# Holding TensorE for a set of score banks, shorter key-value sums, and another order in the last layer

## The chip, the cores and the metric

The kernel runs on one core of a Trainium2 chip. The metric is the device time of one execution in microseconds (us), and smaller is better. TensorE (PE) multiplies matrices and writes PSUM, a memory of eight banks of 512 fp32 columns; ScalarE (ACT) computes functions such as exp and ln; VectorE (DVE) does elementwise work; GpSimd (POOL) and SyncE (SP) do small things and issue DMAs. Each engine takes its instructions in the order in which the program wrote them, and waits at an instruction for the semaphores of others.

## The reference

Four layers are applied to x of 2048 positions and 512 features, each as `x = x + layer(layernorm(x))`. Layers 0 and 2 are attention with 32 query heads of 16 features and one shared key and value head; layers 1 and 3 are linear attention with 32 heads. Cut to what matters:

```python
def A(x, wq, wk, wv, wo):              # layers 0 and 2, S = 2048, H = 32, Dh = 16
    q, k, v = heads(x @ wq), x @ wk, x @ wv
    scores = einsum("bhqd,bkd->bhqk", q, k) * Dh ** -0.5
    return merge(einsum("bhqk,bkd->bhqd", softmax(scores), v)) @ wo

def B(x, wqkv, wo):                    # layers 1 and 3
    q, k, v = split(x @ wqkv)
    pq, pk = phi(q), phi(k)            # phi(t) = where(t > 0, t + 1, exp(t)) + 1e-6
    kv = einsum("bhsd,bhse->bhde", pk, v)
    z = einsum("bhsd->bhd", pk)
    num = einsum("bhqd,bhde->bhqe", pq, kv)
    den = einsum("bhqd,bhd->bhq", pq, z)[..., None] + 1e-6
    return merge(num / den) @ wo
```

## The kernel before

**The plan.** The order of the instructions is not written by hand. The kernel's Python holds a planner (class `Planner`) that plays the whole program through on a clock of its own, with a cost written beside each operation (so 0.22 us for a score product, 0.051 + 0.4267 n for an exponential of n banks), and writes down for each engine the order in which operations were begun. An operation is created by `op`, which finds what it depends on, and has a priority; a smaller number goes first. Whenever an engine is free in the plan, `_dispatch1` takes the ready operation of the best priority. On the chip the engines follow these orders, with semaphores between them; the plan's clock itself is not on the chip. Steps that need a buffer are generators that ask a pool for it ("acq") and go on when they get it; `banks` is the pool of single PSUM banks, `sets` that of the score sets.

**An attention layer** (`run_a`). Positions are cut into 16 tiles of 128. For a query tile, a parity, a key tile and one of four head groups there is one block of scores, 128 keys by 512 columns; the layer has 2048 blocks. Two sets of three PSUM banks (banks 0 to 2 and 3 to 5) take turns. `act_stream` makes a round: it acquires the set that comes free (L1047 and after), lets PE write two or three blocks into it (`qk_mm`, L926, four rows of the array side by side, priority 0), and lets ACT turn two or three banks into probabilities PT in one call (L1107). PT has eight buffers. When DVE's backlog is small, the third bank goes to DVE (`dve_split`, `dve_take`): it turns the scores into an approximate exponential by one addition whose int16 result is read as bf16 (L1194), and makes three shifted copies for a chunk of up to four blocks (L1236), which are combined with fixed weights. A set is free again when ACT's call, and DVE's where there is one, are done. Bank 7 and others that are free are used in the same way for blocks of DVE alone (`alone`).

The value products (`pv_post`, `pv_try`, L980, four columns of the array side by side, priority 2.0) add up PT and DVE's results in bank 6 (`ACC`), tile by tile; DVE copies the sum out (L1259, L1261), PE transposes it (L1278), DVE divides (L1285, L1289), and the output projection and the residual addition follow. Next to all that, PE makes the projections of the neighbouring layers piece by piece (L672, L840). When PE has nothing to do in the plan, `fill` (L1025) and `fill_lin` (L911) put in matmuls on zeros that nobody reads.

A score product and a value product use the array in different modes, "row" and "col"; the planner charges 0.107 us (`SWITCH`) for a change. After the last exponential the sets are given back as single banks.

**A linear layer** (`run_b`) is worked into the attention layer before it as its tiles come: keys and values of a tile (`tile_`), phi (L1363 on ACT, L1364 and L1366 on DVE), queries (`q_`). `kv_` (layer 1) and `kvt` (layer 3) add pk times v, and the sum z, over groups of four tiles (the last groups three and one): the sums of a group are one PE operation of up to 16 matmuls per bank (L1477, L1480 and L1608), added into `kvacc` by DVE.

**The end of layer 3.** When the last tile's sums are there, DVE masks z into the block-diagonal Zbd (L1497) and kv into kvT (L1501); `mix` multiplies kvT with the output weights into four matrices M, copied from PSUM by ACT, DVE, DVE and ACT (L1517, `MCOP`). `den3` makes the denominators of one or two tiles: a product with Zbd (L1542), ln on ACT (L1545), exp of minus that on ACT (L1549, priority 0.02 ahead of the logarithm's by `EXB`), and the product with the query on DVE (L1553). `main3` multiplies by M (L672), DVE adds the residual (L1572), and SP stores the tile. Pairs of banks for `den3` are claimed by `take_pairs`, when the last sums are done.

Of the kernel before, what the change touches and what calls it, by code (L numbers as in the profile page):

```python
# [35 lines left out]
class Planner:  # L36
# [3 lines left out]
    def __init__(self, nc):  # L40
        self.nc = nc
        self.now = 0.0
        self.events = []
        self.seq = 0
        self.ready = {e: [] for e in ENGS}
        self.busy = {e: False for e in ENGS}
        self.until = {e: 0.0 for e in ENGS}
        self.order = {e: [] for e in ENGS}
        self.writer = {}
        self.readers = {}  # L50
        self.flags = {}
# [8 lines left out]
        self.near = {e: [] for e in ENGS}  # L60

    def soon(self, e, o, dur):
# [78 lines left out]
    def _dispatch(self, e):  # L141
        self._dispatch1(e)
        if e == PE and not self.busy[e] and self.idle:
            self.due = [t for t in self.due if t > self.now]
            for f in self.idle:
                f()
        if e == DV and self.hungry and (not self.ready[DV] or self.backlog(DV) < DXB):
            self.hungry[0]()

    def _dispatch1(self, e):  # L150
# [4 lines left out]
        while h:  # L155
# [9 lines left out]
            if w:  # L165
                held.append(x)
                self.at(w, lambda: self._dispatch(e))
                break
            if e == PE and STICK and o.mode != "row" and o.mode != self.mode != "row":
                like = [y for y in h if y[2].eng is None and y[2].mode == self.mode and y[0] <= o.prio + STICK]  # L170
                if like:
                    y = min(like)
                    h.remove(y)
                    heapq.heapify(h)
                    held.append(x)
                    o = y[2]
                    dur, fn = o.opts[e]
            if o.port:
                self.port = self.now + dur
# [264 lines left out]
EXB = 0.02  # L444
# [4 lines left out]
MCOP = (AC, DV, DV, AC)  # L449
# [9 lines left out]
def bass_interleave_layers__grouped_kv_mqa__linear_attn_block__prompt_kernel(  # L459
# [36 lines left out]
    ve = sb("ve", [P, T], FP32)  # L496
    rs = sb("rs", [P, T], FP32)
# [396 lines left out]
    lin = {"a": False, "done": False, "next": -1.0}  # L894

    def fill_lin():
        if pl.busy[PE] or ("x", 3, T - 1) in pl.flags:
            return
        b = ACC
        if lin["a"]:  # L900
# [16 lines left out]
    def run_a(L):  # L917
# [113 lines left out]

        def act_stream():
# [12 lines left out]
            while True:  # L1045
                s_ = yield ("acq", sets, 0.0)
                group = []  # L1047
# [61 lines left out]
                ex.begun = lambda n=n: pl.due.append(pl.now + 0.051 + 0.4267 * n + 0.17)  # L1109
# [138 lines left out]
        def norms():  # L1248
# [17 lines left out]
            lin["a"] = False  # L1266

# [89 lines left out]
    def run_b(L):  # L1357
# [76 lines left out]
        def q_(t):  # L1434
            pr = QBASE + 0.02 * t if QBASE and t >= CRIT else base(t) + 0.01 * t + 0.2
            yield ("flag", ("xnT", L, t))
# [3 lines left out]
            s_ = yield ("acq", bq_pool, pr)  # L1440
            b = yield ("acq", banks, pr)
# [5 lines left out]
        def kvt(gi, ts):  # L1447
# [19 lines left out]
            for i, (c, n) in ((1, parts[1]), (0, parts[0])):  # L1467
# [4 lines left out]
                def fn(e, i=i, b=b):  # L1472
                    ins = None
                    for g in range(4):
# [9 lines left out]
                op({PE: ((0.04 if i else 0.07) * 4 * len(ts), fn)}, reads=rd, writes=[B_(b)], prio=pr, lat=0.2).cols = (16 if i else 512) * len(ts)  # L1484
# [9 lines left out]
            if end:  # L1494
                mk = mask8[:, :, 0:DH]
                v4 = lambda x: x.rearrange("p g (h c) -> p g h c", c=DH)
                o = op({DV: (0.6, lambda e, b=bs[1]: e.tensor_tensor(  # L1497
                    out=v4(Zbd), in0=bank(b, 4).unsqueeze(2).unsqueeze(3).to_broadcast([P, 4, 8, DH]), in1=mk.unsqueeze(1).to_broadcast([P, 4, 8, DH]), op=ALU.mult))},
                       reads=["mask8"], writes=[B_(bs[1]), "Zbd"], prio=pr, after=[("FB", 11, 0)])
# [4 lines left out]
                pl.give_after(banks, bs[0], [o])  # L1504
                for g in range(4):
                    pl.process(mix(g))
            pl.flag(("kv", L, gi))

        Zbd = FB[:, 11, 0:512].rearrange("p (g c) -> p g c", c=P)
        kvT = FB[:, 11, 512:1024].rearrange("p (g c) -> p g c", c=P)  # L1510

        def mix(g):
            pr = 1.45 + 0.001 * g
            b = yield ("acq", banks, pr)
            mm(bank(b), [(kvT[:, g, :], wo2[:, g, :])], ["kvT", "wo2"], b, pr, 0.216)
            dst = FB[:, 0, g * 512:(g + 1) * 512]
            by = {AC: (0.48, lambda e: e.copy(dst, bank(b))), DV: (0.6, lambda e: e.tensor_copy(dst, bank(b)))}  # L1517
            c = op({MCOP[g]: by[MCOP[g]]} if MCOP else by, writes=[B_(b), ("FB", 0, g), ("M", g)], prio=pr)
            pl.give_after(banks, b, [c])
            pl.flag(("M", g))  # L1520

        def take_pairs():
            yield ("flag", ("kv", L, len(KVG) - 1))
            claim(PAIRS, "pair")

        def den3(ts):
# [4 lines left out]
            yield from until(*[("QT", t) for t in ts], "Zbd")  # L1531
# [6 lines left out]
            for k, t in enumerate(ts):  # L1538
# [5 lines left out]
                op({PE: (0.23, fn)}, reads=[("QT", t), "Zbd"], writes=[bk[k]], prio=pr, lat=0.2).cols = 512  # L1544
# [4 lines left out]
            op({AC: (0.148 + 0.427 * n, lambda e: e.activation(rb, rd, ACTF.Exp, scale=-1.0))}, reads=[("rd", i)], writes=[("rb", i)], prio=pr - EXB, after=[("PT", i)])  # L1549
# [27 lines left out]
        def kv_(gi, ts):  # L1577
# [19 lines left out]
            for gs in ((0, 1, 2), (3,)):  # L1597
# [6 lines left out]
                def fn(e, gs=gs, b=b):  # L1604
                    ins = None
                    for i, g in enumerate(gs):
# [3 lines left out]
                    return ins  # L1610
                rd = [("pk", t % 8) for t in ts] + [("va", t % 8) for t in ts] + [("sacc", u) for u in sorted({2 + t % 8 // 2 for t in ts})]
                o = op({PE: (0.08 * len(gs) * len(ts), fn)}, reads=rd, writes=[B_(b)], prio=pr, lat=0.2)
                o.cols = 136 * len(gs) * len(ts)
# [203 lines left out]
```

## Time and profile before

| | us |
|---|---|
| median of 3 runs | 1493.5 (1492.58 to 1494.95) |
| the profiled execution, its own time | 1491.57 |
| its span, first to last instruction | 1489.8 |
| ACT busy, in the span | 1455.9 |
| DVE busy | 1439.1 |
| PE busy, with the matmuls on zeros | 1420.3 |
| first and last attention exponential begin | 9.0 and 1453.4 |

The profile lists groups of instructions as line, engine, operation, what is written and read, shapes and count; behind the first bar the time in which at least one of the group ran and the mean length of one in ns; behind the second the idle time of the engine just before them and who ended it. An instruction's record can overlap the next one of its engine, so waits that are shorter than the overlap do not appear as idle time. In the time line, a line begins with the start and the length in us. A view by windows gives each engine's busy time in a stretch.

### The profile page before, as it was taken

The page shows a single profiled execution, that of the slowest core. Times are in us where ns is not written, and L with a number is a line of the kernel's source. Part 1 is how long each engine was busy: PE and PEld are TensorE (multiplying, and loading weights), DVE is VectorE, ACT ScalarE, POOL GpSimd, SP SyncE. Part 2 cuts the span into 40 slices and gives each one's busy share as a digit, 9 for nine tenths or more (in the row PEclk, how much of TensorE's full clock was granted, in tenths as well). Part 3 has the DMA queues.
Part 4 walks back from the last instruction along what each step waited for, and adds up shares of the span by engine and source line. Part 5 has one row for each costly group of instructions (what it writes and reads, how often), then busy time and mean ns, then how long its engine had stood idle before and what let it go on. Part 6 is the DMA issues. An engine that isn't in the chain of part 4 may idle for free.

```text
span 1489.8 us, 36266 instructions
## 1 busy us (share of the span) xinstructions
PE 1420.3 (95%) x14792; PEld 515.5 (35%) x14792; DVE 1439.1 (97%) x2679; ACT 1455.9 (98%) x1443; POOL 77.2 (5%) x155
## 2 busy tenths in 40 slices
PE   8999999999999999999999999999999999999999
PEld 4423333323323333323733333333333333333336
DVE  8899999999999999999879999999999999999996
ACT  8999999999999999999799999999999999999996
POOL 5000000000000000000022000000000000000000
PEclk9999999999999999999999999999999999999999
DMA  5100000000000000000031000000000000000001
GB/s 125 62 9 8 9 8 6 9 8 5 9 9 9 9 5 5 2 1 2 2 48 39 2 12 9 12 9 9 5 9 5 9 9 9 8 2 2 1 2 58
DMA packets 53540, 20.71 MB, mean 14 GB/s; under 512 B 47232, under 2 KB 52864, under 8 KB 53376
## 3 DMA queue, kind: packets, MB, share of 16 engines
q1 hardware_dynamic: 52320, 18.36, 5.7%
q8 instruction: 118, 1.93, 0.5%
q14 instruction: 46, 0.38, 0.1%
q10 hardware_dynamic: 1056, 0.03, 0.0%
HBM read 5.28 MB, written 2.10 MB: 5 GB/s over the span
## 4 chain that ended last, share of the span: by engine, by line
PE 21%; ACT 14%; DVE 10%; issue 5%; DMA 1%; DVEq 0%; ACTq 0%
ACT PT L1107 13%; PE ps L980 7%; PE ps L926 6%; DVE FB L1194 5%; DVE FB L1236 3%; PE ps L672 3%; PE ps L1025 2%; PE ps L840 1%; PE ps L1278 1%; DMA xnT<-xn 1%; PE ps L911 0%; ACT phE L1363 0%; DVE sacc L1259 0%; DVE QT L1366 0%; DVE st L754 0%
## 5 line engine op out<-in xcount | busy, mean ns | idle before, releaser
L1107 ACT ACTIVATE PT<-ps 128x1024 bf16<-128x1024 f32 (+1 forms) x1309 | 1399.7, 1230 | 3.9 <-PE ps L926 2.5
L1194 DVE TENSOR_SCALAR FB<-ps 128x512 int16<-128x512 f32 x1046 | 687.3, 679 | 7.0 <-PE ps L926 4.4
L926 PE MATMUL ps<-QT,KM 32*128 32x512 bf16 x4096 | 530.4, 385 | 30.3 <-ACT PT L1107 23.4
L980 PE MATMUL ps<-FB,VW 128*32 128x512 bf16 x4184 | 528.0, 385 | 16.8 <-ACT PT L1107 6.3
L1236 DVE TENSOR_SCALAR FB<-FB 128x2048 int16<-128x2048 int16 x786 | 515.3, 676 | 0.4
L980 PE MATMUL ps<-PT,V 128*32 128x512 bf16 x3050 | 482.1, 386 | 13.0 <-ACT PT L1107 9.9
L926 PEld LDWEIGHTS ps<-QT,KM 32*128 32x128 bf16 x4096 | 133.4, 91 | 433.7 <-ACT PT L1107 303.4
L980 PEld LDWEIGHTS ps<-FB,VW 128*32 128x32 bf16 x4184 | 132.1, 94 | 184.4 <-issue 83.9
L1025 PE MATMUL ps<-QT,V 128*32 128x512 bf16 (+6 forms) x758 | 178.3, 312 | 1.6 <-DVE FB L1194 1.6
L980 PEld LDWEIGHTS ps<-PT,V 128*32 128x32 bf16 x3050 | 120.7, 94 | 128.2 <-issue 60.1
L1025 PEld LDWEIGHTS ps<-QT,V 128*32 128x32 bf16 x758 | 60.3, 95 | 81.1 <-issue 51.7
L672 PE MATMUL ps<-wqkv,xnT 128*128 128x512 bf16 (+1 forms) x272 | 77.2, 372 | 0.0
L745 POOL TENSOR_TENSOR rs<-ve,mhalf 128x1 f32<-128x1 f32 x59 | 43.1, 732 | 579.6 <-DVE ve L743 575.3
L743 POOL TENSOR_SCALAR ve<-mv 128x1 f32<-128x1 f32 x32 | 14.7, 458 | 674.0 <-DVE mv L755 673.8
L1363 ACT ACTIVATE phE<-ps 128x512 bf16<-128x512 f32 (+1 forms) x66 | 42.3, 642 | 7.1 <-PE ps L840 5.5
L1278 PE MATMUL ps<-identF,sacc 128*128 128x128 f32 x256 | 46.8, 291 | 0.8 <-DVE sacc L1259 0.8
L1259 DVE COPY sacc<-ps 128x512 f32<-128x512 f32 x64 | 43.5, 679 | 1.3 <-PE ps L980 1.1
L754 DVE BATCH_NORM_STATS2 st<-x_sb 128x6 f32<-128x512 bf16 x60 | 40.5, 679 | 2.1 <-DMA x_sb<-in_A_x_dram 1.9
L840 PE MATMUL ps<-xnT,wqkv 128*128 128x128 bf16 x512 | 38.8, 220 | 0.0
L672 PE MATMUL ps<-wo,OT 128*128 128x512 bf16 x120 | 37.4, 385 | 0.0
L840 PE MATMUL ps<-xnT,wq 128*128 128x128 bf16 x464 | 36.3, 221 | 0.9 <-DVE FB L1194 0.4
L1278 PEld LDWEIGHTS ps<-identF,sacc 128*128 128x128 f32 x256 | 27.4, 141 | 22.2 <-issue 13.5
(138 smaller groups left out, 640.5 us busy)
## 6 DMA issues: line engine op xcount, KB each, us to landing
out_dram<-x_sb SPq DMA_DIRECT2D x16, 128.0 KB, 1.7
x_sb<-in_A_x_dram SPq DMA_DIRECT2D x6, 256.0 KB, 4.2
wqkv<-in_B_wqkv_dram SPq DMA_DIRECT2D x1, 1536.0 KB, 8.9
xnT<-xn SPq DMA_TRANSPOSE x48, 2.4
x_sb<-in_A_x_dram SPq DMA_DIRECT2D x4, 128.0 KB, 2.5
wq<-in_A_wq_dram SPq DMA_DIRECT2D x1, 512.0 KB, 4.1
wo<-in_A_wo_dram SPq DMA_DIRECT2D x1, 512.0 KB, 4.1
wo<-in_B_wo_dram SPq DMA_DIRECT2D x1, 512.0 KB, 9.6
```

What stands on the lines that cost most here:

```text
L672: return e.matmul(dst, lhsT=l, rhs=r, start=(k == 0), stop=(k == len(pairs) - 1))
L745: op({PO: (0.55, lambda e: e.tensor_tensor(out=rs[:, t:t + 1], in0=ve[:, t:t + 1], in1=mhalf[:], op=ALU.pow))}, reads=[("ve", t), "mhalf"] ...
L840: ins = e.matmul(dst[:, g * P:(g + 1) * P], lhsT=lhs(g, k), rhs=rhs(k), start=(k == 0), stop=(k == FT - 1))
L926: return e.matmul(bank(b), lhsT=KM[r, sg.par, kt * P:(kt + 1) * P], rhs=QT[r, sg.t, :], start=True, stop=True)
L980: ins = e.matmul(ps[32 * j:32 * j + 32, ACC * 512:(ACC + 1) * 512], lhsT=V[:, kt, :] if w is None else VW[:, kt, w, :], rhs=ap, start=(k = ...
L1025: o = op({PE: (n / 2400.0, lambda e: e.matmul(ps[32 * j:32 * j + 32, b * 512:b * 512 + n], lhsT=V0[:], rhs=QT[:, sg.t, 0:n], start=st, sto ...
L1107: ex = op({AC: (0.051 + 0.4267 * n, lambda e, n=n, s_=s_, p_=p_: e.activation(PT[:, p_, 0:n * 512], ps[:, s_ * 512:(s_ + n) * 512], ACTF.E ...
L1194: o = op({DV: (0.602, lambda e: e.tensor_scalar(out=dst.bitcast(I16), in0=bank(b), scalar1=VB, scalar2=VLO, op0=ALU.add, op1=ALU.max))}, w ...
L1236: o = op({en: (du, lambda e, w=w, g_=g_: e.tensor_scalar(out=FB[:, g_, 0:n].bitcast(I16), in0=FB[:, f_, 0:n].bitcast(I16), scalar1=float(w ...
L1259: o = op({DV: (0.6, lambda e, src=src: e.tensor_copy(src, bank(ACC)))}, writes=[B_(ACC), key], prio=0.0, lat=0.15)
L1278: o = op({PE: (0.12, lambda e, c=c: e.transpose(ps[:, b * 512 + c * P:b * 512 + (c + 1) * P], src[:, c * P:(c + 1) * P], identF[:]))}, rea ...
L1363: op({AC: (0.07 + n / 1200.0, lambda e: e.activation(phE[:, i, 0:n], bank(b, n), ACTF.Exp))}, reads=[B_(b)], writes=[("phE", i)], prio=pr ...
```

## The change

PE's dispatcher in the plan gets a new rule. When an exponential begins, `act_stream` now records a "turn": the time at which its set will be free, and the latest time at which scores must begin so that the exponential after the next one is not late. When PE would begin an operation other than a score product, `yields` looks at the turns: if a set comes free within 0.2 us (`HMAX`) and the operation would end later than the scores may begin, by more than 0.3 (`HK`) of the time to be waited, the operation is held until 5 ns after the release. During a hold the matmuls on zeros are not put in either (`keep`).

```diff
+    def yields(self, dur):
+        self.turns = [x for x in self.turns if x[0]() > self.now - 0.004]
+        for rel, late in self.turns:
+            r = rel()
+            if r < self.now + HMAX and self.now + dur - max(r, late()) > HTOL + HK * max(0.0, r - self.now):
+                return max(r, self.now) + 0.005
+        return 0.0
...
-        if e == PE and not self.busy[e] and self.idle:
+        if e == PE and not self.busy[e] and self.idle and self.now >= self.keep:
...
+            if e == PE and o.mode != "row" and o.prio < 9.0:
+                w = self.yields(dur + (max(0.0, SWITCH - (self.now - self.until[e])) if self.mode != o.mode else 0.0))
+                if w:
+                    self.keep = w
+                    held.append(x if x[2] is o else y)
+                    self.at(w, lambda: self._dispatch(e))
+                    break
...
-                ex.begun = lambda n=n: pl.due.append(pl.now + 0.051 + 0.4267 * n + 0.17)
+                def begun(n=n, s_=s_, p1=p1 if split is not None else None):
+                    e1 = pl.now + 0.051 + 0.4267 * n
+                    pl.due.append(e1 + 0.17)
+                    nx = rounds.get(3 - s_)
+                    d = nx[1] if nx and nx[0].eng is None else 0.904
+                    turn = (lambda: max(e1 + EX_LAT, 0.0 if p1 is None else p1.end or p1.due or 1e9), lambda: e1 + d - QK_LAT - SWITCH)
+                    pl.turns.append(turn)
+                    rounds[s_] = (ex_[s_], 0.0, turn)
```

The key-value sums become an operation for each head group of 128 features instead of one for all (layer 3: four pieces; layer 1: three and one); the matmuls are the same:

```diff
-                op({PE: ((0.04 if i else 0.07) * 4 * len(ts), fn)}, reads=rd, writes=[B_(b)], prio=pr, lat=0.2).cols = (16 if i else 512) * len(ts)
+                for gs in (((0, 1, 2, 3),) if i or not KSP else ((0,), (1,), (2,), (3,))):
+                    op({PE: ((0.04 if i else 0.07) * len(gs) * len(ts), lambda e, gs=gs, fn=fn: fn(e, gs))}, reads=rd, writes=[B_(b)], prio=pr, lat=0.2).cols = (4 if i else 128) * len(gs) * len(ts)
```

In the last layer the order changes. All four M are copied by DVE; the products that make M have a higher priority (1.3 for 1.45). Zbd is made from a copy `zs` of z, in four pieces, the first on ACT and three on DVE, instead of one DVE operation. The exponentials of `den3` go 0.35 ahead of the logarithms for tiles up to 3, and behind them by 0.05 for the others. The query of tile 15 gets priority 1.9 instead of 1.78, and the pairs of banks are claimed when it asks for its bank. Bank 6 is lent to the pool when layer 2's last sums are copied out.

```diff
-EXB = 0.02
+EXB = -.05
...
-MCOP = (AC, DV, DV, AC)
+MCOP = (DV,)*4
...
+            if L == 2 and LEND:
+                lin["lent"] = True
+                plain_give(banks, ACC)
...
+            if t in QLAST and L == 3:
+                pr = QLP
...
+            if L == 3 and t == T - 1 and QCL:
+                claim(PAIRS, "pair")
...
+                o = op({DV: (0.08, lambda e, b=bs[1]: e.tensor_copy(zs[:], bank(b, 4)))}, writes=[B_(bs[1]), "zs"], prio=pr - 0.05)
                 pl.give_after(banks, bs[1], [o])
+                for g in range(4):
+                    op({AC: (0.19, lambda e, g=g: e.activation(v4(Zbd)[:, g], mk, ACTF.Copy, scale=zs[:, g:g + 1]))} if g in ZAC else
+                       {DV: (0.11, lambda e, g=g: e.tensor_scalar(out=v4(Zbd)[:, g], in0=mk, scalar1=zs[:, g:g + 1], scalar2=None, op0=ALU.mult))},
+                       reads=["mask8", "zs"], writes=[("Zbd", g)], prio=0.5 if g in ZAC else pr - 0.05, over=[("FB", 11, 0)])
...
         def mix(g):
-            pr = 1.45 + 0.001 * g
+            pr = MIXP + 0.001 * g
...
-            op({AC: (0.148 + 0.427 * n, lambda e: e.activation(rb, rd, ACTF.Exp, scale=-1.0))}, reads=[("rd", i)], writes=[("rb", i)], prio=pr - EXB, after=[("PT", i)])
+            op({AC: (0.148 + 0.427 * n, lambda e: e.activation(rb, rd, ACTF.Exp, scale=-1.0))}, reads=[("rd", i)], writes=[("rb", i)], prio=pr - (EXF if ts[0] < EXN else EXB), after=[("PT", i)])
```

More of the change, by code (lines that the diff above doesn't have):

```diff
@@ L443 @@
 CLB = (3, 4)
-EXB = 0.02
+EXB = -.05
+LEND = True
+MBF = False
+ZAC = (0,)
+EXF = 0.35
+EXN = 4
+QCL = True
+QLAST = (15,)
+QLP = 1.9
+TPF = ("kv", 3, 4)
+MIXP = 1.3
 PAIRS = (0, 1, 4, 5)
@@ L892, in bass_interleave_layers__grouped_kv_mqa__linear_attn_block__prompt_kernel @@
     kicks = {}
-    lin = {"a": False, "done": False, "next": -1.0}
+    lin = {"a": False, "lent": False, "done": False, "next": -1.0}
     def fill_lin():
@@ L899, in fill_lin @@
         b = ACC
-        if lin["a"]:
+        if lin["a"] or lin["lent"]:
             if not lin["done"]:
@@ L1030, in run_a @@
         pl.idle.append(fill)
+        rounds, ex_ = {}, {}
         def act_stream():
@@ L1046, in act_stream @@
                 s_ = yield ("acq", sets, 0.0)
+                if s_ in rounds and rounds[s_][2] in pl.turns:
+                    pl.turns.remove(rounds[s_][2])
                 group = []
@@ L1470, in kvt, with fn @@
                 b = bs[i]
-                def fn(e, i=i, b=b):
+                def fn(e, gs, i=i, b=b):
                     ins = None
-                    for g in range(4):
+                    for g in gs:
                         for t in ts:
@@ L1504, in kvt @@
                 pl.give_after(banks, bs[0], [o])
+            pl.flag(("kv", L, gi))
+            if end:
                 for g in range(4):
                     pl.process(mix(g))
-            pl.flag(("kv", L, gi))
+        ZK = [("Zbd", g) for g in range(4)]
         Zbd = FB[:, 11, 0:512].rearrange("p (g c) -> p g c", c=P)
@@ L1530, in den3 @@
                 yield ("flag", ("bq", L, t))
-            yield from until(*[("QT", t) for t in ts], "Zbd")
+            yield from until(*[("QT", t) for t in ts], *ZK)
             i = yield ("acq", rd_pool, pr)
```

37 lines of the change are left out of this document (23 added, 14 removed).

## The prediction

> **What bounds the kernel now.** I read the page's engine shares first, then the costliest groups, the same groups by shape, the time line of one late round, and last the windows and the time line of the end.
>
> ```profile
> PE 1420.3 (95%) x14792; PEld 515.5 (35%) x14792; DVE 1439.1 (97%) x2679; ACT 1455.9 (98%) x1443; POOL 77.2 (5%) x155
> ...
> L1107 ACT ACTIVATE PT<-ps 128x1024 bf16<-128x1024 f32 (+1 forms) x1309 | 1399.7, 1230 | 3.9 <-PE ps L926 2.5
> L1194 DVE TENSOR_SCALAR FB<-ps 128x512 int16<-128x512 f32 x1046 | 687.3, 679 | 7.0 <-PE ps L926 4.4
> ...
> L1236 DVE TENSOR_SCALAR FB<-FB 128x2048 int16<-128x2048 int16 x786 | 515.3, 676 | 0.4
> ```
>
> ScalarE (ACT) and VectorE (DVE) share the exponentials of both attention layers: 4096 blocks of 512 columns, 1046 on DVE, 3050 on ACT. Both look full, and only 3.9 us of idle time stand before ACT's exponentials, so a change that makes scores come sooner seems to have nothing to win. The groups by shape say otherwise:
>
> ```profile
> L1107 ACT ACTIVATE PT<-ps 128x1024 bf16<-128x1024 f32 x875 | 863.9, 1092 | 1.9 <-PE ps L926 1.4
> L1107 ACT ACTIVATE PT<-ps 128x1536 bf16<-128x1536 f32 x433 | 630.1, 1510 | 1.9 <-PE ps L926 1.2
> ```
>
> In the trace's single instructions, the commonest distance from one exponential's start to the next is 903 ns after a two-bank one and 1330 ns after a three-bank one. 875 x 0.903 + 433 x 1.330 + one of 0.476 is 1366.5 us, and the page has 1399.7 us busy. The records overlap (a two-bank record is at least 1018 ns long), so up to 0.12 us of waiting vanishes between them. Start to start, 403 of 1252 back-to-back rounds are late by over 5 ns: 25.9 us in all, 24.4 us of it in 317 rounds behind a two-bank exponential. Here is one such round, first TensorE's (PE's) line, then ACT's:
>
> ```profile
> 668.79 0.40 PE L980 MATMUL ps<-PT,V 128*32 128x512 bf16 x4
> 669.13 0.40 PE L926 MATMUL ps<-QT,KM 32*128 32x512 bf16 x4
> ```
>
> ```profile
> 669.57 1.45 ACT L1107 ACTIVATE PT<-ps 128x1536 bf16<-128x1536 f32 x1
> ```
>
> The exponential before it starts at 668.36, so this one was due at 669.26 and comes 0.31 late. The exponential that ended at 668.74 released two things at once: its probabilities (what L980 multiplies) and its score banks (what L926 fills). The value product went first; the scores started 0.33 later, and the exponential 0.44 after them, which is the least this trace has between the two.
>
> **How the 25.9 us divide** (PE's pieces in progress when the older exponential's release arrives, 54 ns behind its end). (a) 104 rounds, 9.8 us: a piece begins within 10 ns of the release, 100 times a value product: the tie just shown. (b) 214 rounds, 7.0 us: one piece began earlier and overruns. (c) 55 rounds, 8.6 us: further pieces are begun after that exponential's release, since the set also waits for DVE's block in it, or much was queued. The rest, 0.5 us, is in rounds whose scores were prompt.
>
> **Part 1, the wait.** Before PE begins anything but scores, the new rule compares its end with the latest start of the coming scores, and holds it if the set comes free within 0.2 us and the overrun is more than 0.3 of the waiting. In (a) waiting costs nothing: scores and value product change places. I take 9.0 of 9.8 us. In (b) I applied the condition to the trace's own distances: 78 rounds pass it, with 4.3 us of lateness and 4.8 us of PE waiting. The plan's clock and the chip's differ, so I take 3.0 us. In (c) the release is often DVE's and known to the plan only once it is scheduled; I take 1.5 us, with the sums of part 2 inside it. Sum 13.5 us of ACT time; bounds 0 and 25.9.
>
> ACT's time is not yet the span's. Blocks go to DVE by its backlog, so both engines stay full and share a saving. A block costs ACT 1366.5/3050 = 0.448 us; DVE 0.601 (start to start) plus 786 x 0.600/1046 = 0.451 for the shifted copies, 1.052 us. ACT's share of the rate is (1/0.448)/(1/0.448 + 1/1.052) = 0.70. So 13.5 x 0.70 = **9.5 us**, bounds 0 and 18.1. DVE also waits for late scores: 13.5 us beyond the usual start-to-start distances stand before L1194 in the two stretches below. I take 2 us x 0.30 = **0.6 us**, bounds 0 and 4.1.
>
> What the wait costs lies on PE. Queued behind a held piece are value products, projections and the fillers of L1025. Who waits for them: the probability buffers (eight) and the layer's later tiles. The fillers do no work:
>
> ```profile
> 60.00:700.00 640.00, 92.35 (x406) 31.89 (x406) 1.00 0.04 6
> 800.00:1440.00 640.00, 77.98 (x327) 26.27 (x327) 1.00 0.03 7
> ```
>
> (these columns: PE, PEld, clock; L1025 alone). With all work PE is busy for 612.1 and 610.1 us of the same stretches, so 58 us idle plus some 142 us of fillers counted start to start are about 200 us of spare PE time, over 1184 exponentials: 0.17 us each. 4.8 us of waiting is nothing beside it. Cost zero; without that cover every 0.01 us per round would be 11.8 us.
>
> **Part 2, shorter runs of key-value sums.** The same matmuls become four pieces, or three, instead of one, so scores can pass between. The trace shows rounds behind L1480, L1608 and L1477 late by 0.42, 0.12 and 0.17 us at worst, 0.8 us in six rounds. It is inside (c). Extra mode changes fall on spare PE time.
>
> **Part 3, the last layer.** The end, from the windows and the time line:
>
> (Columns: PE, PEld, DVE, ACT, POOL.)
>
> ```profile
> 1465.70:1482.90 17.20, 17.20 (x162) 10.99 (x160) 13.80 (x29) 17.05 (x20) 0.00 (x0) 1.00 0.21 70
> ```
>
> ```profile
> 1466.31 0.58 ACT L1517 CAST FB<-ps 128x512 bf16<-128x512 f32 x1
> ...
> 1467.32 0.58 ACT L1517 CAST FB<-ps 128x512 bf16<-128x512 f32 x1
> ...
> 1469.50 0.69 DVE L1572 TENSOR_TENSOR x_sb<-x_sb,ps 128x512 bf16<-128x512 bf16 x1 [1.25 <-PE ps L672]
> 1470.90 0.76 DVE L1553 TENSOR_TENSOR FB<-PT,QT 128x512 bf16<-128x512 bf16 x2 [0.70 <-ACT PT L1549]
> ```
>
> ACT is busy 17.05 of 17.20 us here, with logarithms (L1545) and exponentials (L1549); after its end DVE still has 4.8 us of products and additions. Moving both mixing copies off ACT takes 0.48 + 0.47 us (start to start) out of its row. DVE gets two copies, 1.2 us, in a place where 1.25 + 0.70 us stand idle. The denominator mask in pieces is worth 0.2 us at most. Putting the first tiles' exponentials first makes ACT wait for each logarithm, some 0.2 us three times, but fills DVE's early gaps; tile 15's query, moved behind, can put 0.5 us back on ACT. A bank lent earlier shows no wait that it would end. Best case: DVE has no gap after 1464.5, 4.3 us idle now less the 1.0 us added, so 3.3 us sooner. Worst: its added 1.2 us are all late. I take **1.0 us** sooner, between -3.3 and +1.2. What is late next is DVE's 0.34 + 0.60 us per tile. No DMA is added and nothing moves past SP's or POOL's queue: the 16 stores (1.7 us each) follow the last additions as now.
>
> **Sum.** 9.5 + 0.6 + 1.0 = 11.1, say 11 us less. The profiled execution took 1491.6 us (span 1489.8 and 1.8 around it), so 1480.6; it lies 1.9 us below the median of the three runs, 1493.5, which is what the result is compared with. Predicted: **1482.5 us**.
>
> **Rivals.** *It does not do what it says:* the plan's clock misjudges the releases, the ties are broken elsewhere, and only part 3 is left: 1493.5 - 1.0 = 1492.5 us. For it: 34% of the lateness is in (c). Against: a tie needs no clock. Chance 0.08.
> *Slower, through PE's spare time:* the rule holds pieces in most rounds, not in the late ones only; value products pile up, the probability buffers run out, and ACT waits for PE. It decides from 0.17 us of waiting per round; at 0.19, under the rule's 0.2, PE is 0.02 x 1184 = 24 us over, less the 11 saved: 1506 us. Against: 4.8 us of waiting by the trace's own distances. For: each held piece may cost two further changes between score and value work, and from value product to scores the trace has 0.33 us where value products follow each other at 0.22. Chance 0.07. The Trainium skill, TensorEngine Tiling (Array Packing), section Key Properties, says that changing the tiling mode drains TensorE; the 0.11 us between these two rows agrees, and by that rule alone the change loses only if it adds changes.
> *The clock falls,* because PE now idles on purpose and the fillers pause. All slices of the page have PEclk at 9 or over and every window shows 1.00; at half of it PE's 1080 us of real work in 1280 would need 2160, so even a twentieth of the time at half clock costs 64 us x 0.69 = 44 us: 1526 us. Against: waits under 0.2 us, where PE has waited 1.3 us (the longest before L926) at 1.00. Chance 0.01. The Trainium skill, TensorE: Matmul & The Clock Gate, Part 1, puts the loss after an idle window of about 3.4 us; no run here shows such a gap.
> *Everything late goes:* all 25.9 us (18.1), DVE's 4.1, part 3's 3.3: 25.5 us less, 1468 us. Against: (c) is not addressed. Chance 0.05.
>
> **Chances and range.** The forecast keeps 0.79. A measurement of this kernel tells about 0.2%, 3 us, from no change: of the forecast's cases 0.03 lie within that. Faster 0.76 + 0.05 = 0.81, the same 0.08 + 0.03 = 0.11, slower 0.08. The range goes down to 1474, where part 1 takes all 25.9 us (18.1) and part 3 its 1.0, and up to 1492.5, where part 3 alone is left; what lies outside has 0.13.
>
> **What would show it.** Right: what the exponentials' distances start to start have beyond 903 and 1330 ns falls from 25.9 to about 12 us; in tied rounds L926 stands ahead of L980; DVE takes fewer than 1046 blocks. From the start of the last attention exponential to the end it is 1 us shorter than now (1453.4 to 1489.8). Wrong: as many late rounds as before, fewer fillers at equal time (waiting without use), or a longer end.

## The result, and the profile after

The changed kernel takes 1498.6 us (median of 21 executions, 1494.4 to 1501.2) where the kernel before takes 1493.0 (21 executions, 1491.7 to 1504.6). The ratio, with disturbed executions left out, is 1.0026, 95% interval [1.0014, 1.0038]: slower by 0.26%, where 0.7% faster was forecast (the medians over all executions are 0.38% apart). The profiled execution took 1498.8 us (span 1497.0). The page of the changed kernel, in the columns used before, with the line of the scores before (L926) below it (the exponential is now L1145, the scores L960, the value product L1014, DVE's blocks L1242):

```profile
PE 1397.7 (93%) x14679; PEld 513.4 (34%) x14775; DVE 1437.0 (96%) x2668; ACT 1458.3 (97%) x1444; POOL 77.2 (5%) x155
...
L1145 ACT ACTIVATE PT<-ps 128x1024 bf16<-128x1024 f32 (+1 forms) x1307 | 1407.3, 1346 | 7.7 <-PE ps L960 4.4
L1242 DVE TENSOR_SCALAR FB<-ps 128x512 int16<-128x512 f32 x1037 | 688.4, 683 | 8.9 <-PE ps L960 4.8
L960 PE MATMUL ps<-QT,KM 32*128 32x512 bf16 x4096 | 530.4, 385 | 72.0 <-ACT PT L1145 55.8
```

```profile
L926 PE MATMUL ps<-QT,KM 32*128 32x512 bf16 x4096 | 530.4, 385 | 30.3 <-ACT PT L1107 23.4
```

Two of the four signs of being right are here: DVE takes 1037 blocks for 1046, and the scores stand ahead in the tied rounds (below). PE waits for ACT ahead of its scores 55.8 us (23.4 before). The other two are not: what the distances start to start have beyond 903 and 1330 ns was to fall from 25.9 to about 12 us and stands at 23.7 (361 late rounds for 403), and from the last attention exponential to the end it takes 1.8 us longer, not 1 us less. The mean exponential's record grew from 1230 to 1346 ns, in both shapes:

```profile
L1145 ACT ACTIVATE PT<-ps 128x1024 bf16<-128x1024 f32 x862 | 883.6, 1203 | 2.5 <-PE ps L960 2.1 <-PE ps L1014 0.2
L1145 ACT ACTIVATE PT<-ps 128x1536 bf16<-128x1536 f32 x445 | 677.6, 1624 | 5.2 <-PE ps L1014 2.9 <-PE ps L960 2.2
```

The same operation, 0.11 us longer, looks like a slower ACT; the first experiment shows that it is the opposite. The tie of the prediction is now broken the other way. PE's time line in the changed kernel has the scores 0.32 us ahead of the value products:

```profile
301.95 0.39 PE L960 MATMUL ps<-QT,KM 32*128 32x512 bf16 x3 [0.40 <-ACT PT L1145]
302.27 0.40 PE L1014 MATMUL ps<-FB,VW 128*32 128x512 bf16 x3
```

Of 104 rounds with a piece begun within 10 ns of the release, 4 are left (9.8 us of lateness before, 0.3 now). Yet the time did not fall. By stages, from the starts of the attention exponentials in the two traces:

| us | layer 0 | between | layer 2 | last exponential's start to the end |
|---|---|---|---|---|
| before | 701.8 | 25.7 | 716.9 | 36.5 |
| after | 700.3 | 26.5 | 722.5 | 38.3 |

Layer 0 gains 1.5 us; layer 2 loses 5.6 and the end 1.8.

### The profile page after: what moved, and what is told of

Its sections match the earlier page's. It is cut to its first block, busy times and chain, and to the rows that moved or that the text cites. A ratio compares the mean times of both kernels' runs of the same rounds, so it can differ in the third digit from the quotient of the medians.

```text
span 1497.0 us, 36247 instructions
## 1 busy us (share of the span) xinstructions
PE 1397.7 (93%) x14679; PEld 513.4 (34%) x14775; DVE 1437.0 (96%) x2668; ACT 1458.3 (97%) x1444; POOL 77.2 (5%) x155
## 4 chain that ended last, share of the span: by engine, by line
PE 37%; ACT 32%; DVE 18%; issue 10%; DMA 1%; POOL 0%; SPq 0%; ACTq 0%
ACT PT L1145 31%; PE ps L1014 13%; PE ps L960 12%; DVE FB L1242 8%; DVE FB L1284 5%; PE ps L706 4%; PE ps L1059 3%; PE ps L874 2%; PE ps L1329 2%; ACT phE L1414 1%; DVE sacc L1307 1%; DMA x_sb<-in_A_x_dram 1%; DVE st L788 1%; DVE xn L797 0%; DVE sacc L1417 0%
## 5 line engine op out<-in xcount | busy, mean ns | idle before, releaser
L1145 ACT ACTIVATE PT<-ps 128x1024 bf16<-128x1024 f32 (+1 forms) x1307 | 1407.3, 1346 | 7.7 <-PE ps L960 4.4
L1242 DVE TENSOR_SCALAR FB<-ps 128x512 int16<-128x512 f32 x1037 | 688.4, 683 | 8.9 <-PE ps L960 4.8
L960 PE MATMUL ps<-QT,KM 32*128 32x512 bf16 x4096 | 530.4, 385 | 72.0 <-ACT PT L1145 55.8
L1014 PE MATMUL ps<-FB,VW 128*32 128x512 bf16 x4148 | 515.7, 385 | 6.8 <-DVE sacc L1307 3.2
L1284 DVE TENSOR_SCALAR FB<-FB 128x2048 int16<-128x2048 int16 (+1 forms) x783 | 514.3, 677 | 0.3
L1014 PE MATMUL ps<-PT,V 128*32 128x512 bf16 x3059 | 458.4, 386 | 0.8 <-ACT PT L1145 0.3
L960 PEld LDWEIGHTS ps<-QT,KM 32*128 32x128 bf16 x4096 | 134.3, 91 | 509.0 <-ACT PT L1145 429.2
L1014 PEld LDWEIGHTS ps<-FB,VW 128*32 128x32 bf16 x4148 | 128.5, 94 | 159.5 <-issue 102.1
L1059 PE MATMUL ps<-QT,V 128*32 128x128 bf16 (+6 forms) x799 | 175.7, 304 | 0.4 <-DVE FB L1242 0.2
L1014 PEld LDWEIGHTS ps<-PT,V 128*32 128x32 bf16 x3059 | 112.8, 94 | 100.7 <-issue 70.3
L1059 PEld LDWEIGHTS ps<-QT,V 128*32 128x32 bf16 x799 | 68.0, 96 | 67.8 <-issue 27.2
L706 PE MATMUL ps<-wqkv,xnT 128*128 128x512 bf16 (+1 forms) x219 | 62.8, 367 | 5.7 <-issue 2.7
L1414 ACT ACTIVATE phE<-ps 128x512 bf16<-128x512 f32 (+1 forms) x66 | 48.3, 734 | 7.0 <-PE ps L874 5.8
L874 PE MATMUL ps<-xnT,wq 128*128 128x128 bf16 x464 | 35.7, 223 | 0.0
L874 PEld LDWEIGHTS ps<-xnT,wqkv 128*128 128x128 bf16 x512 | 29.4, 98 | 9.2 <-issue 5.8
```

Of the source, the lines that this page charges most:

```text
L706: return e.matmul(dst, lhsT=l, rhs=r, start=(k == 0), stop=(k == len(pairs) - 1))
L874: ins = e.matmul(dst[:, g * P:(g + 1) * P], lhsT=lhs(g, k), rhs=rhs(k), start=(k == 0), stop=(k == FT - 1))
L960: return e.matmul(bank(b), lhsT=KM[r, sg.par, kt * P:(kt + 1) * P], rhs=QT[r, sg.t, :], start=True, stop=True)
L1014: ins = e.matmul(ps[32 * j:32 * j + 32, ACC * 512:(ACC + 1) * 512], lhsT=V[:, kt, :] if w is None else VW[:, kt, w, :], rhs=ap, start=(k = ...
L1059: o = op({PE: (n / 2400.0, lambda e: e.matmul(ps[32 * j:32 * j + 32, b * 512:b * 512 + n], lhsT=V0[:], rhs=QT[:, sg.t, 0:n], start=st, sto ...
L1145: ex = op({AC: (0.051 + 0.4267 * n, lambda e, n=n, s_=s_, p_=p_: e.activation(PT[:, p_, 0:n * 512], ps[:, s_ * 512:(s_ + n) * 512], ACTF.E ...
```

## The experiments

Times "at clock 1.000" are read from a straight line through one kernel's executions, time over mean granted clock: executions of the same program differ in that clock (0.994 to 1.000 for the changed kernel), and every 0.001 costs about 1.1 us (1494.5 us at 1.000, 1498.6 at 0.997, 1501.1 at 0.994). For the kernel before, five sets of executions give 1491.6 to 1492.1 by this line; 1492.1 is used below.

**What a late exponential is.** ACT alone: 120 two-bank exponentials, then 80 three-bank, then 40 two-bank, back to back, with nothing to wait for but the one eight before; the run computes no layer and stores zeros.

```python
for n, m in ((2, 120), (3, 80), (2, 40)):
    for i in range(m):
        ...
        ins = e.activation(PT[:, k % 8, 0:n * 512], ps[:, s * 512:(s + n) * 512], ACTF.Exp, scale=0.0054, bias=0.0)
```

> No layer is computed (the output is zeros): ACT alone does 120 exponentials of two banks, 80 of three and 40 of two, back to back, with nothing to wait for but its own call eight before. Theory A (a call can begin sooner than its predecessor's work allows; the ends set the rate): the records grow from about 1.02 us to a largest length of about 1.37 and the ends stand 915 and 1342 ns apart throughout; the starts stand 903 and 1330 apart at first and 915 and 1342 later. If 903 and 1330 are the engine's true rates: both starts and ends stay 903 and 1330 apart and the records keep their length.

Its time line, ACT's calls in one row and the store that waits for the last of them:

```profile
5.61 254.21 ACT L26 ACTIVATE PT<-ps 128x1024 bf16<-128x1024 f32 x240
...
259.91 7.74 SPq L39 DMA_DIRECT2D out_dram<-x  x16
```

160 x 0.9165 + 80 x 1.3435 = 254.1 us, and that is what it took; the *ends* of the records stand 916.5 and 1343.5 ns apart throughout. The *starts* stand 903 and 1330 ns apart throughout, which would have given 250.9. So each record of an uninterrupted row begins about 13 ns earlier against its end than the one before it, without limit: the first is 1005 ns long, the last 4181, and the means of the groups are absurd:

```profile
L26 ACT ACTIVATE PT<-ps 128x1024 bf16<-128x1024 f32 x160 | 149.5, 2320 | 0.0
L26 ACT ACTIVATE PT<-ps 128x1536 bf16<-128x1536 f32 x80 | 109.1, 3547 | 0.0
```

The store begins 0.09 us behind the last end, so the ends are the true ones. A long record means a row that was not interrupted, and 903 and 1330 were never ACT's rate. By ends, the kernel before loses 10.0 us, not 25.9: of the difference, 1308 calls x 12 ns (915 - 903, the distances of ends and starts in that trace) = 15.7 us is the lead that late starts give back without delaying anything. That is also why the changed kernel, with 9.2 us lost by ends, still shows 23.7 by starts. The forecast's cap on the record's growth and its slower starts in a long row were wrong too.

**Only the ties.** The plan of before, and in PE's finished order 177 tied pairs change places:

```diff
+            if v.mode == "row" and v.prio == 0.0 and u.mode == "col" and u.prio == 2.0 and u not in v.deps and abs(v.el - u.t0) < 0.004:
+                q[i - 1], q[i] = v, u
```

> The kernel before with its plan untouched; only in PE's finished order 177 pairs are exchanged, where a value product and a score product became ready at the same instant of the plan and the value product stood first (the tie of the prediction's case a). ACT's and DVE's orders and shares stay as they were. Theory D (the prediction's: each late start of an ACT call is lost): the 9.8 us of case (a) come off ACT, 6 to 9 us off the span, 1484 to 1487 us. Theory A (absorbed: ACT can begin a call every 903 ns but end one only every 915, so a late start eats a lead of up to 0.3 us first, and only the 10.0 us that the ends lose can be won at all): lateness start to start falls by some 9 us, the ends lose 5 to 8 us instead of 10.0, and the time moves by 0 to 3 us, 1490 to 1493 us.

1492.9 us, ratio 0.9995 [0.9978, 1.0011]: no change. Tied rounds fall from 104 to 6 (from 110 to 23 when 10 ns to either side are counted), but the lateness start to start stays at 25.4 us (357 rounds); it only turns up elsewhere, and by ends 8.9 us are lost (10.0 before). The ends change by 1.1 us and the time by less than its interval. So the 9.0 us taken for the ties, the largest term of the sum, is not to be had.

**The wait, taken away and put in alone.** Two runs ask what the wait does: the changed kernel without it, and the kernel before with it alone. (A small part of the rule, that no matmul on zeros is put in while an older rule, `soon`, holds PE, stays in the first and comes with the second.)

```diff
-HMAX = 0.2
+HMAX = -9.0
```

> The changed kernel without its wait (the 0.2 us look-ahead set to -9, so that nothing is ever held); shorter sums and the new last layer stay. Theory 1 (the clock: by waiting, PE falls below the activity that keeps its clock at full; 0.997 granted in the profiled execution, 0.994 to 1.000 over the 21 executions, 1501 to 1494.5 us): granted clock 1.000 in all executions, executions within 3 us of each other, median 1490 to 1494 us. Theory 2 (late starts of ACT's calls were mostly absorbed by the overlap of its calls, so that the wait had little to give): the calls' ends lose about 10 us beyond 915 and 1342 ns as in the kernel before (9.2 in the changed one). Theory 3 (the new last layer is what costs: from the last attention exponential to the end 38.3 us for 36.5): still 38 us and a median near 1495 us.

> The kernel before with the wait alone; sums and last layer as before. Theory 1 (clock): granted clock below 1.000 in more than half of the executions, a spread of 4 us or more with the clock, median 1494 to 1499 us. Theory 2 (absorbed): in executions at clock 1.000 the time is 1490 to 1492 us, 1 to 2 us better than before and no more. Theory 3 (last layer): the wait by itself is no loss, median 1491 us or less, and 36 to 37 us from the last attention exponential to the end.

Without the wait 1497.0 us, 1.0021 [1.0008, 1.0033]; with it alone 1503.5 us, 1.0062 [1.0047, 1.0076]. The two do not add up to a story: taken out of the one kernel, the wait hardly matters, and put into the other it costs 10 us, in layer 2 (727.8 us) and in the end (39.3). Without the wait the clock is 0.999 or more in 11 of 12 executions, as the theory of the clock had it, but the time is not the 1490 to 1494 us that went with it. The granted clock was 0.999 to 1.000 in the second run, so the clock is not what it costs there.

That asks how far the order itself scatters. The planner is greedy, and any number in it redraws everything behind. So four edits that ought to mean nothing, in kernels with and without the wait:

```diff
-QK_DUR = 0.22
+QK_DUR = 0.2199
```

(or 0.2205, or `PV_DUR` 0.2223 for 0.222), and one that books the exponential by the distance of its ends:

```diff
-                ex = op({AC: (0.051 + 0.4267 * n, ...
+                ex = op({AC: (0.061 + 0.427 * n, ...
...
-                    d = nx[1] if nx and nx[0].eng is None else 0.904
+                    d = nx[1] if nx and nx[0].eng is None else 0.915
```

Before with `QK_DUR` 0.2199 and with `PV_DUR` 0.2223:

> The kernel before with nothing changed but one number of the plan: a score product is booked at 0.2199 us instead of 0.22. No work is added, taken away or held; only ties in the plan fall otherwise. Theory E (the order is a draw: a plan that is made greedily comes out otherwise with any small change, and the kernel before has a lucky one): 4 to 7 us slower than before, 1497 to 1500 us, most of it in layer 2, at a granted clock like before's. If order is no cause: 1493 us, within 1 us.

> The same with another number: a value product is booked at 0.2223 us instead of 0.222. Theory E (a draw): a second, different time, 1496 to 1501 us. If order is no cause: 1493 us, within 1 us.

1496.0 us, 1.0028 [1.0015, 1.0041], and 1500.6 us, 1.0049 [1.0035, 1.0062]. Nothing was changed that a programmer would call a change, and one is as far from before as the result is, the other farther. Both lose it in layer 2 (721.5 and 722.8 us for 716.9). The same two with the wait alone:

> The wait alone in the kernel before (old sums, old last layer), with the score product booked 0.2199 instead of 0.22 us in the plan; its partner without the wait is e6 (1495.3 us at full clock). Theory 'the wait is worth about 4 us whatever the draw, and e2 was one bad draw': 1488 to 1496 us at full clock, layer 2 near 720 us. Theory 'the wait harms unless the key-value sums are cut, because a long piece that is held moves on and delays value products': slower than e6 by 5 to 11 us, 1500 to 1506 us, and from the last exponential to the end over 39 us as in e2.

> The same wait alone in the kernel before, with the value product booked 0.2223 instead of 0.222 us; its partner without the wait is e7 (1500.6 us median). Theory 'worth about 4 us whatever the draw': 1493 to 1500 us at full clock. Theory 'harms with long sums': 1505 to 1511 us. If one of the two runs gains and the other loses by several us, the pairs only scatter, and the wait's worth is smaller than what one draw of the order moves.

1498.4 us, 1.0034 [1.0016, 1.0051], and 1496.9 us, 1.0019 [1.0002, 1.0036]: one loses, the other gains against its partner. So the run with the wait alone looks like a bad draw, and a rule that the old sums make the wait harmful is not borne out. The changed kernel with `QK_DUR` 0.2199, then that without the wait:

> The changed kernel with a score product booked at 0.2199 us instead of 0.22. Theory E: another draw of the changed kernel, 1489 to 1497 us for 1498.6; if it lies below the kernel before while the two neutral versions of before lie above it, then the change does gain and was only compared with a lucky order. If order is no cause: 1498 us, within 1 us at the same clock.

> The version e8 (changed kernel, score product booked at 0.2199 us) without the wait. If the wait is worth what the ends of ACT's calls lose (10.0 us without it, 5.6 with it in e8, of which 0.70 reach the span): 2 to 4 us slower than e8's 1490.4 at clock 1.000, 1493 to 1495 us. If the draw rules: anything from 1490 to 1500 us.

1490.6 us, 0.9984 [0.9976, 0.9993], and 1497.7 us, 1.0031 [1.0018, 1.0044]. With `QK_DUR` 0.2205, without and with the wait:

> The changed kernel without the wait, a score product booked at 0.2205 us. With the wait worth 2 to 4 us: that much above e15 at clock 1.000. If the draw rules: either sign, up to 6 us.

> The changed kernel with its wait, a score product booked at 0.2205 us. Another draw: 1490 to 1497 us at clock 1.000; 2 to 4 us below e14 if the wait is worth that.

1497.1 us, 1.0027 [1.0014, 1.004], and 1500.3 us, 1.0042 [1.0026, 1.0057]. With the new booking: with the wait at 0.22, then at 0.2199, and the latter without the wait:

> The changed kernel with one cost of the plan corrected: an exponential of n banks is booked at 0.061 + 0.427 n (0.915 and 1.342 us, as its ends stand) instead of 0.051 + 0.4267 n (0.904 and 1.331). Theory F (in the changed kernel the plan charges ACT too little, so ACT gets too many blocks and DVE stands idle at layer 2's end, 4.55 us before L1547): DVE's longest idle time there falls below 2.5 us, and at clock 1.000 the time is 1 to 4 us below the changed kernel's 1494.5, as far as the draw of the order (some 2 us either way) allows. If the charge is no cause: DVE still stands idle for 4 us or more there.

> The same with a score product booked at 0.2199 us instead of 0.22, another draw of the order. Theory E (draw): differs from the version before it by 2 to 7 us, 1486 to 1491 us. Theory F (charge): DVE's longest idle time at layer 2's end is below 2.5 us here too.

> The version e11 (exponentials booked as their ends stand, score product at 0.2199 us) without the wait. With the wait worth 2 to 4 us: 1489 to 1491 us at clock 1.000 for e11's 1486.9. If the draw rules: either sign, up to 6 us.

1495.5 us, 1.002 [1.0009, 1.0031]; 1489.5 us, 0.9972 [0.9961, 0.9983], faster than both kernels; and 1494.6 us, 1.001 [1.0001, 1.002]. The theory that the end would shorten with the true booking fell: DVE idles 3.8 and 5.3 us at the end of layer 2 in the first two, where the old booking had 4.6 and 4.2. With one draw on either side of each edit, whether the new booking itself gains stays open.

The seven pairs that differ in the wait alone (without it -> with it; lost by ACT: what the distances of the exponentials' ends have beyond 915 or 916 and 1342 or so, the tenth percentile of each trace; DVE: the same for its blocks beyond 601 ns, inside the two layers):

| pair | us at clock 1.000 | lost by ACT, us | rounds over 20 ns late | lost by DVE, us |
|---|---|---|---|---|
| before, wait alone | 1492.1 -> 1502.5 | 10.0 -> 7.7 | 79 -> 26 | 12.4 -> 24.4 |
| the same, 0.2199 | 1495.3 -> 1497.1 | 12.7 -> 7.0 | 87 -> 22 | 11.2 -> 26.0 |
| the same, 0.2223 | 1499.5 -> 1496.4 | 14.7 -> 5.7 | 103 -> 23 | 13.0 -> 19.2 |
| changed kernel | 1496.8 -> 1494.7 | 10.9 -> 9.2 | 86 -> 25 | 13.5 -> 19.2 |
| the same, 0.2199 | 1495.6 -> 1490.4 | 10.9 -> 5.6 | 84 -> 16 | 11.4 -> 19.4 |
| the same, 0.2205 | 1496.8 -> 1495.1 | 10.8 -> 11.5 | 79 -> 21 | 18.0 -> 27.7 |
| 0.2199, new booking | 1494.6 -> 1486.9 | 12.7 -> 4.9 | 109 -> 18 | 9.9 -> 10.4 |

The last three columns are the steady ones. In every pair the wait removes two thirds or more of ACT's late rounds, 90 -> 22 in the mean, and in six of seven it saves ACT time, 4.4 us of 11.8 in the mean. And in every pair DVE's blocks come later, by 8.1 us in the mean (12.8 -> 20.9; by 0.5 in the last pair). DVE's group in the third pair, without and with the wait (both executions at a granted clock of 1.000):

```profile
L1194 DVE TENSOR_SCALAR FB<-ps 128x512 int16<-128x512 f32 x1042 | 687.6, 682 | 7.3 <-PE ps L926 5.4
```

```profile
L1230 DVE TENSOR_SCALAR FB<-ps 128x512 int16<-128x512 f32 x1035 | 685.6, 683 | 9.1 <-PE ps L948 6.0
```

What shows as idle time grows by 1.8 us, end to end by 6.2: overlapping records hide the rest, as on ACT. The counts in these two lines, 1042 and 1035, show where ACT's saving goes: in every pair DVE takes fewer blocks with the wait, 7 to 16, in the mean 9.9. The blocks are dealt out in the plan, and what DVE doesn't take is ACT's. At 0.453 us each by ends (1382 us for 3050 blocks in the kernel before) 9.9 blocks are 4.5 us more for ACT to do, as much as the 4.4 it no longer loses, while DVE has less to do and waits longer. With the prediction's own shares, 4.4 x 0.70 = 3.1 us are won on ACT and 8.1 x 0.30 = 2.4 given back on DVE. The time itself scatters more than that: the pairs give +10.4, +1.8, -3.1, -2.1, -5.2, -1.7 and -7.7 us, mean -1.1, with a 95% interval of about +-5.5 (standard deviation 5.9, seven pairs). The wait's own worth cannot be told from nothing.

**The last layer's order.** The changed kernel with the old constants of the last layer (the mask Zbd stays in four pieces, all on DVE):

```diff
-EXB = -.05
-LEND = True
-ZAC = (0,)
-EXF = 0.35
-QCL = True
-QLAST = (15,)
-MIXP = 1.3
-MCOP = (DV,)*4
+EXB = 0.02
+LEND = False
+ZAC = ()
+EXF = 0.02
+QCL = False
+QLAST = ()
+MIXP = 1.45
+MCOP = (AC, DV, DV, AC)
```

> The changed kernel with the last layer's order of the kernel before (priorities, copies and bank claims; the mask for z stays in pieces, all four on DVE); the wait and the shorter sums stay. Theory 3 (last layer): 2 to 3 us faster than the changed kernel, 1495 to 1496 us, and 36.5 us from the last attention exponential to the end. Theory 1 (clock): granted clock 0.994 to 1.000 as in the changed kernel, median 1497 to 1500 us. Prediction's part 3 (the new order is worth 1 us): 1 us slower than the changed kernel at the same clock.

1499.0 us, 1.0033 [1.0022, 1.0045]; 1496.3 at clock 1.000, 1.6 us above the changed kernel's 1494.7, which one pair of draws can't tell from nothing. Over all traces, from the last exponential's start to the end:

| us, mean (runs) | without the wait | with the wait |
|---|---|---|
| old last layer | 36.8 (before, ties, two neutral: 36.5, 36.5, 36.7, 37.6) | 38.3 (39.3, 36.2, 37.8, old order 39.8) |
| new last layer | 35.7 (35.6, 35.6, 35.5, 36.0) | 37.4 (after 38.3, then 36.0, 36.6, 38.2, 37.9) |

The new order takes 0.9 to 1.1 us off in the means, and the wait puts 1.5 to 1.7 on. The runs without the wait lie close together on either side; those with it scatter by up to 3.6 us. Where the time goes is seen at the end of layer 2, on DVE in the kernel before, then on DVE and on PE in the changed one:

```profile
1452.13 0.68 DVE L1236 TENSOR_SCALAR FB<-FB 128x2048 int16<-128x2048 int16 x1
1454.56 0.29 DVE L1364 TENSOR_SCALAR phE<-phE 128x512 bf16<-128x512 bf16 x1 [1.74 <-ACT phE L1363]
```

```profile
1454.31 2.50 DVE L1284 TENSOR_SCALAR FB<-FB 128x2048 int16<-128x2048 int16 x6
1461.35 0.16 DVE L1547 TENSOR_TENSOR kvacc<-kvacc,ps 128x4 f32<-128x4 f32 x1 [4.55 <-PE ps L1532]
```

```profile
1460.87 0.44 PE L1532 MATMUL ps<-va,sacc 128*128 128x1 bf16 x12
1461.18 0.83 PE L1535 MATMUL ps<-sacc,va 128*128 128x128 bf16 x12
1461.84 0.39 PE L874 MATMUL ps<-xnT,wqkv 128*128 128x128 bf16 x4
1462.16 0.40 PE L1014 MATMUL ps<-PT,V 128*32 128x512 bf16 x3
```

DVE has nothing for 4.55 us (1.74 before), and the last value product (L1014) comes behind sums and projections of layer 3. The longest such gap of DVE is 4.2 us in the mean of the nine traces with the wait (1.3 to 5.4) and 2.4 in seven without it (1.3 to 4.0). How the wait leads to it is not shown.

**The clock.** The profile after has a mean granted clock of 0.997, where before had 1.000. Windows of the changed kernel (PE, PEld, DVE, ACT, POOL, clock), one ahead of the fall and one in it:

```profile
1023.48:1026.90 3.42, 2.10 (x24) 0.64 (x20) 3.42 (x8) 3.42 (x5) 0.00 (x0) 1.00 0.00 0
1026.93:1030.34 3.41, 3.13 (x26) 0.84 (x26) 2.85 (x5) 2.91 (x3) 0.00 (x0) 0.50 0.02 5
```

There are three half-clock pieces of 3.41 us in layer 2 of that trace, two of them in a row from 743.6. To see whether sparse PE work does it, the plan of before with the matmuls on zeros (L1025) taken out of PE's finished order:

```diff
+        gone = {o for o in self.order[PE] if o.prio == 9.0 and o.mode == "col"}
+        self.order[PE] = [o for o in self.order[PE] if o not in gone]
```

> The kernel before with its plan untouched, but the matmuls on zeros of the attention layers (L1025) taken out of PE's finished order; every other instruction stands where it stood. Theory 1 (the clock falls when PE is too little busy in a window of some 3.4 us, and costs 1.0 to 1.2 us per 0.001 of mean clock): clock 0.95 to 0.98 and 1512 to 1545 us. If the clock does not depend on them: 0.998 and 1492 us, or a little less, since 39 late rounds stood behind a filler.

1545.8 us, 1.0354 [1.0329, 1.0379], at clock 0.946 in the profile, and ACT loses 62.9 us by ends. The slices of this run's page:

```profile
PEclk9989989899899889999998999999999998899999
```

So the clock falls when PE is thinly used, and the price is about the same: the profiled execution takes 51.9 us more than the 1492.5 us of the kernel before beside it, for 0.054, or 0.96 us per 0.001. The wait is not shown to lower the clock: over the seven pairs the mean of all executions is 0.9987 without and 0.9982 with it. The changed kernel's 0.997 differs from 0.9994 in its neutral edit with `QK_DUR` 0.2199, so it goes with the order drawn.

What matmuls on zeros during a hold would do stays open: the run that lets them in (e3) gave no result, because in its order a matmul adds to a bank in which no sum is open.

## Why the prediction was wrong, point by point

- **"Start to start, 403 of 1252 rounds are late: 25.9 us in all."** This is the step that failed. The base was the distance of starts; ACT's rate is that of ends, 12 to 13 ns longer. The true loss was 10.0 us, and the prediction took 13.5 us out of it.
- **Part 1, "I take 9.0 of 9.8 us" for the ties, 3.0 and 1.5 for the rest.** The ties went as foretold (104 -> 4) and brought nothing: when they alone were swapped, the time kept. The wait as a whole saves ACT 4.4 us by ends in the mean, 1.7 in the changed kernel itself.
- **"Blocks go to DVE by its backlog, so both engines stay full and share a saving."** The backlog is the plan's. With the wait the plan gave ACT 9.9 blocks more in the mean, 4.5 us, and DVE on the chip stood waiting instead of sharing. That DVE takes fewer than 1046 blocks came true, and is no sign of a gain.
- **"DVE also waits for late scores", 0.6 us to win.** The sign was wrong: DVE's blocks lose 8.1 us more in the mean, 2.4 us by its share. Why PE's holds make its scores later than the plan has them, no run shows.
- **"4.8 us of waiting is nothing", cost zero.** Not quite: ahead of its exponentials ACT stands idle behind value products for 3.0 us in the changed kernel, in four waits, and for none in the kernel before (0 to 3.6 us in the other traces with the wait, 0 to 2.3 without). That is far from the 24 us of the rival on PE's spare time, which fell. A cost also came where the prediction had not looked, at the end: 1.5 to 1.7 us with late value products.
- **Part 2, inside (c).** No gain to be seen: without the wait, layer 2 takes 723.5, 722.9 and 722.0 us with the shorter sums, and 716.9, 721.5 and 722.8 with the old ones.
- **Part 3, 1.0 us sooner.** Right in size: 1.1 between the runs without the wait, 0.9 with more scatter between those with it. Which of its edits gives it, no run shows.
- **"The clock falls", chance 0.01, 44 us.** The mechanism exists at a smaller price: half clock for some 10 us of the profiled execution. The 1.3 us named there as PE's longest wait before L926 is that of the weight loads; the matmuls' own is 1.0.
- **What no step had: the order is a draw.** At clock 1.000 the three orders of the kernel before, it and its two neutral edits, take 1492.1, 1495.3 and 1499.5 us, mean 1495.6; the changed kernel's, in five bookings, 1494.7, 1490.4, 1495.1, 1494.2 and 1486.9, mean 1492.3. So the difference of 2.6 us at clock 1.000 is -3.3 between the means, 3.5 that before lay under its mean, and 2.4 that the changed kernel lies over its own. Another 3.0 us is the clock: the medians stand 3.9 and 0.9 us above the time at 1.000. That makes 5.6, the difference of the medians. The -3.3 has a standard error of 2.7 and is not shown to differ from zero. Two of the five orders have the new booking; the other three alone have a mean of 1493.4. That before was a lucky draw rests on three orders.

## What to carry to other kernels

Measure the lateness of a busy engine on the ends of its records, or on what waits for them, never on starts that can run ahead: here it shrank from 25.9 to 10.0 us. Where a greedy planner writes the order, run a few neutral edits of both kernels before an effect under 0.5% is believed, and compare at equal granted clock. A rule that favours one of two engines which share the work must be priced on the other as well, and at the end, where there is nothing left to hide it.

## What the runs showed of the hardware

An ACT record's start can run ahead of the work: 903 and 1330 ns from start to start, 916.5 and 1343.5 from end to end, over 240 calls, with records of 1.0 to 4.2 us. The granted clock halves in pieces of 3.41 us, in the changed kernel with no idle time of PE over 0.94 us in the records ahead of them. In the window from 1023.48, shown above, PE has five sets of score or value products at 0.22 us each and 0.3 us of matmuls on zeros: it streamed columns for 0.41 of the time. The window ahead of 743.6 comes to about 0.45 when 512 columns are counted as 0.22 us, and to 0.50 when its smallest products are counted at their distances. Before's thinnest window had 0.48 and kept the clock, and one at 0.45 in the changed kernel kept it as well, so the two cases show no boundary. The Trainium skill, TensorE: Matmul & The Clock Gate, Part 1, puts the fall behind an idle window of about 3.4 us. The length agrees with 3.41; the window was not idle here, and the measurement decides.
